# Two attention layers on one core: where the values of a step stand when an output product stands in it

## The chip, the cores and the metric

The kernel runs on one core of one Trainium2 chip. The metric is the device time of one execution in microseconds; of several runs the median is taken. A profile of one execution is at hand as well. In it PE is TensorE, PEld its weight loads, DVE is VectorE, ACT is ScalarE, POOL is GpSimd and SP is SyncE.

## The reference

Two attention layers run over two inputs of 2048 positions and 576 channels. Each has 32 heads of 18 channels. Their outputs stand side by side.

```python
def _A_ref(x, wqkv, wo):                 # local, dilated: 8 keys, 2 apart, back from the query
    ...
    logits = jnp.einsum("bhsd,bhswd->bhsw", q, kg) * scale
    attn = _softmax(jnp.where(mask[None, None, :, :], logits, -1e9), axis=-1)
    o = jnp.einsum("bhsw,bhswd->bhsd", attn, vg)
    return o.transpose(0, 2, 1, 3).reshape(B, S, D) @ wo

def _B_ref(x, wqkv, wo):                 # full attention
    ...
    p = _softmax(jnp.einsum("bhqd,bhkd->bhqk", q, k) * scale, axis=-1)
    o = jnp.einsum("bhqk,bhkd->bhqd", p, v)
    return o.transpose(0, 2, 1, 3).reshape(B, S, D) @ wo

return jnp.concatenate([a, b], axis=-1)
```

All tensors are float32.

## The kernel before

The work has three stages. First come the projections of both layers (to about 420 us). Then comes a long row of equal steps for the full attention of layer B, with layer A's local attention worked in beside it. The last part is an end with the last output products. The change touches the row of steps.

**A step.** There are 512 steps: 8 groups of 4 heads, in each 4 blocks of 512 queries, in each 16 tiles of 128 keys (`kt`). The order of instructions on each engine is the order in which the Python code issues them; a manual schedule is set, so nothing is moved afterwards. In a step TensorE does:

- four **scores** (`score`, matmul on L269): 128 keys by 512 queries, one for each head, of float32r. Heads 0 and 2 use the upper 64 rows of the array, heads 1 and 3 the lower 64, so that one of each kind run side by side. The order is `for h in (0, 2, 1, 3)`. ScalarE makes exponentials of each (`e`, L276).
- **maxima** for later blocks (`block`, matmul `take` on L158): scores of queries by keys, of which VectorE takes the maximum (`reduce`, L166, result `mx`). A step holds two whole ones (`maximum(1)` behind the first score, `maximum(0)` behind the last) and one in two halves of 256 columns that share one bank (`parts_of_maximum`). So three banks are reduced in each step. On VectorE the reduce of `maximum(1)` stands first, that of the two halves second, that of `maximum(0)` third.
- four **values** (`weigh`, L739): the exponentials of the step before, times the values `v`, summed into one bank `po` over 16 steps. Each is 19 columns wide, and the four stand in four column groups of the array. Each shows as two matmul records, so a step has eight.

**Banks.** `po` keeps one of eight PSUM banks. The other seven are handed out by `bank(kind)` in rings: the ring "scores" has banks 0 to 3, the ring "else" has banks 4 to 6. Each call gives the next bank of its ring; the matmul that writes it first waits until the bank's last reader is done.

**Output products.** When a part of a layer's attention is done, it is multiplied with `wo` (`beside`, matmul on L1058): two sums of 288 columns, `one` on the upper 64 rows and `two` on the lower, 13 or 14 matmuls each for layer A (27 in all), which run side by side. `one` takes a bank of the ring "scores", `two` one of "else". Two more maxima are put between its matmuls. `sums_of_a` does it for layer A (32 times), `sum_of` for layer B. A product that is due waits in the list `inside`, and the next step takes it in: before, just ahead of the step's last score (`h == 3`). In such a step the bank of `maximum(1)` is asked for first of all (`ps = bank() if inside and whole else None`), ahead of the bank of the two halves. Afterwards ScalarE copies one sum to `y` (L973) and VectorE adds the other (L974; issued from the list `behind_scores`).

**Values and exponentials.** At the end of each step the step before is weighed (`weigh(ready.pop(0))`), so two steps' exponentials are alive at once: eight tiles of 2 KB a partition, six in the pool `e_room` and two in `work`. Near the end, when there are no maxima left (`paired`), the values of two steps stand together.

**GpSimd's transfers.** 36 transfers are issued by GpSimd (L140, L141) in the projections; their descriptors lie in a scratch room of 16 KB a partition.

Of the kernel before, what the change touches and what calls it, by code (L numbers as in the profile page):

```python
# [7 lines left out]
F32 = mybir.dt.float32  # L8
F32R = mybir.dt.float32r
BF16 = mybir.dt.bfloat16  # L10
AF = mybir.ActivationFunctionType
# [22 lines left out]
ALL = NG * STEPS  # L34
# [25 lines left out]
def two_attentions(ctx: ExitStack, tc, xa, wa, woa, xb, wb, wob, out):  # L60
# [5 lines left out]
    nc = tc.nc  # L66
# [13 lines left out]
    def bank(kind=None):  # L80
        r = rings[kind or ring]
        r.append(r.pop(0))
        return p_bank.tile([128, 512], F32, name=f"bank{r[-1]}")
# [22 lines left out]
    step = 0  # L106
# [8 lines left out]
    def due():  # L115
        for f in agenda.pop(step, []):
            f()
# [89 lines left out]
    def settle():  # L207
        while owing:
            owing.popleft()()
# [7 lines left out]
    def next_piece(r):  # L217
        n, i = divmod(given[r], PIECES)
        given[r] += 1
        if n not in blocks:  # L220
            blocks[n] = block(*divmod(n, NB))
        return blocks[n], (r, i // 2 // NB, i // 2 % NB, i % 2)

    def maximum(r, ps=None):

        ps = ps or bank()
        (take, reduce), piece = next_piece(r)
        take(ps, *piece)
        return lambda: reduce(ps, *piece)
# [9 lines left out]
    def parts_of_maximum():  # L239

        if not begun:
            both = [next_piece(r) for r in range(2)]
            assert both[0][1][1:] == both[1][1][1:]
            begun.extend((both, part) for part in range(2))
        both, part = begun.popleft()
        ps = bank()
        one = both[1][0][0](ps, *both[1][1], part)

        between = nc.scalar.nop()
        sync(between, one)  # L250

        def other():
            (take, reduce), piece = both[0]
            sync(take(ps, *piece, part), between)
            reduce(ps, *piece, part)

        return other

    e_room = None
    counted = [-1]  # L260

    def score(g, b, kt, h, kind="scores", between=None):

        assert (g, b) in placed
        qs, ks = sets[g % 3]
        p, r = divmod(h, 2)
        ps = bank(kind)
        at = slice(64 * r, 64 * r + 56)
        nc.tensor.matmul(ps, ks[at, p, 128 * kt : 128 * kt + 128], qs[at, b, p], start=True, stop=True)  # L269
        if between:  # L270
            between()

        counted[0] += 1
        early = counted[0] % 8 < 6
        e = (e_room if early else work).tile([128, 512], F32, name="e", bufs=6 if early else 2)
        nc.scalar.activation(e, ps, AF.Exp, scale=SCALE)  # L276
        return e

# [26 lines left out]
    def halves(r, odd, w, x, wcols, xcols, weights_move=False):  # L305

        at = slice(64 * r, 64 * r + 64)
        both = [p for c in range(4) for p in pairs(c, w, x, wcols, xcols)] + pairs(4, w, x, wcols, xcols)[: 1 + (r == odd)]
        return [(b[at], a[at]) if weights_move else (a[at], b[at]) for a, b in both]
# [68 lines left out]
    with (tc.tile_pool(name="x", bufs=1, side="right") as xp,  # L378
# [4 lines left out]
        early = ExitStack()  # L383
# [98 lines left out]
        if True:  # L482
# [34 lines left out]
            for c in range(5):  # L517
                one, other = (load, nc.scalar.dma_start) if c % 2 == 0 else (nc.scalar.dma_start, load)
# [79 lines left out]
            for t in range(NT):  # L598
                ps = bank()
# [94 lines left out]
            for t in order[:4]:  # L694
                ps = bank()
# [34 lines left out]
        step = 0  # L730
# [3 lines left out]
    work = ctx.enter_context(tc.tile_pool(name="work", bufs=1, reuse_waits="tile"))  # L734
    ring = "else"
    def weigh(*steps):
        for g, b, kt, es in steps:
            for i in range(4):
                nc.tensor.matmul(po[32 * i : 32 * i + 19], vs[g][:, kt, 19 * i : 19 * i + 19], es[i],  # L739
                                 start=kt == 0, stop=kt == NT - 1)  # L740
        if kt == NT - 1:
            finish(g, b)
# [116 lines left out]
    def local(j):  # L859
# [102 lines left out]
        def finished(h, n):  # L962
            inside.append(lambda: sums_of_a(h, n))

        def sums_of_a(h, n):
            his, los = zip(*wo["a"])
            w = his[:4], los[:4], his[4], los[4]
            cols = slice(288 * h, 288 * h + 288)
            if h == 0:
                st["y"] = ys["a", j, n] = work.tile([128, D], F32, name="y", bufs=4)  # L970
            one, two = beside("scores", *(halves(r, 0, w, st["x", n], cols, slice(0, 128), True) for r in range(2)))
            y = st["y"][:, cols]
            nc.scalar.activation(y, two, AF.Copy)  # L973
            behind_scores.append(lambda: nc.vector.tensor_add(y, one, y))  # L974


        soon = 0 if j else 3
# [60 lines left out]
    behind_scores = []  # L1038

    inside = []  # L1040
# [3 lines left out]
    def beside(kind, *both):  # L1044

        sums_ = [bank(k)[:, :288] for k in (kind, None)]
        turns = [[(sums_[r], *ab, i == 0, i == len(t) - 1) for i, ab in enumerate(t)] for r, t in enumerate(both)]
        pair = kind and sum(given) + 2 <= NG * NB * PIECES * 2
        if pair:

            for r in range(2):
                turns[r].insert(6 + 4 * r, None)
        for i in range(max(map(len, turns))):
            for r in range(2):
                if i < len(turns[r]):
                    if turns[r][i]:
                        ps, a, b, start, stop = turns[r][i]
                        nc.tensor.matmul(ps, a, b, start=start, stop=stop)  # L1058
                    else:
                        maximum(r)()  # L1060
        if pair:

            rings["else"].append(rings["else"].pop(0))
        return sums_

    def sum_of(y, t, h, chunks, kind=None):

        pos, cols = slice(128 * t, 128 * t + 128), slice(288 * h, 288 * h + 288)
        both = []
        for r in range(2):  # L1070
            both.append([])
            for c, (hi, lo) in enumerate(chunks):
                at = slice(64 * r, min(64 * r + 64, hi.shape[0]))
                whi, wlo = wo["b"][c]
                both[r] += [(a[at, pos], w[at, cols]) for a, w in ((hi, whi), (hi, wlo), (lo, whi))]
        one, two = beside(kind, *both)
        if kind:
            nc.vector.tensor_copy(y, one)
        else:
            nc.scalar.activation(y, one, AF.Copy)  # L1080
        nc.vector.tensor_add(y, two, y)

    def first(t, b, h):
        sums[t, b, h] = bank()[:, :288]
# [40 lines left out]
    def partial(t, h):  # L1125

        b = NB - 1
        if h == 0:
            name = ("aq", "ao", "aohi")[t]
            ys["part", t] = work.tile([128, DH, SUB], F32, name=name, bufs=1)  # L1130
        y = ap(ys["part", t], (1, DH * SUB))[:, 288 * h : 288 * h + 288]
        waiting.append(lambda: sum_of(y, t, h, olds[b]))
        sums[t, b, h] = (y,)
# [22 lines left out]
    ready = [(0, 0, 0, es)]  # L1156
    early = sum(given)
# [4 lines left out]
    paired = False  # L1162
    due()
    step += 1
    while step < ALL:
        n, kt = divmod(step, NT)
        g, b = divmod(n, NB)
        es = [None] * 4

        whole = total - sum(given) > 1  # L1170
        parts = (bool(begun) or total - sum(given) > 3) and step not in copied

        ps = bank() if inside and whole else None


        ahead = kt == 0 and (n < 6 or n >= 24)
        part = [parts_of_maximum()] if parts and not ahead else []
        for h in (0, 2, 1, 3):

            if inside and h == 3:  # L1180
                inside.pop(0)()
            es[h] = score(g, b, kt, h, between=(lambda: part.append(parts_of_maximum())) if parts and ahead and h == 0 else None)
            if h == 0 and whole:
                maximum(1, ps)()
            if h == 1 and parts:
                part[0]()
            if h == 3 and whole:
                maximum(0)()
        if sum(given) == total and not begun:
            settle()  # L1190
        for fs in (behind_scores, outside):
            while fs:
                fs.pop(0)()

        paired = paired or kt % 2 == 0 and sum(given) == total and not begun
        for _ in range(1 if paired and step < ALL - 2 else len(waiting)):
            if waiting:
                waiting.pop(0)()
        if ready and (kt % 2 == 0 or not paired):
            weigh(ready.pop(0))  # L1200
        ready.append((g, b, kt, es))
        if paired and kt % 2:
            weigh(*ready)
            ready.clear()
        due()

        if len(waiting) > (0 if not paired else 2 if kt % 2 else len(waiting)):
            waiting.pop(0)()
        step += 1
# [24 lines left out]
```

## Time and profile before

| what | value |
|---|---|
| time, median of 3 runs | 1603.24 us (1603.08 to 1604.28) |
| span of the profiled execution | 1603.8 us; the page gives no other time for this execution |
| mean granted clock of TensorE | 0.998 |
| PE busy | 1590.0 us (99%) |
| DVE busy | 1383.7 us (86%) |
| ACT busy | 1217.7 us (76%) |
| POOL busy | 960.1 us (60%) |

The shares are means over stages. In the projections ACT is busy for 15 to 43 us of each 80 us; in the row of steps PE has 79 to 80 us of each 80, ACT 75 to 79 and DVE 74 to 76. In a row of the timeline the first number is the start in microseconds from the span's start, the second the duration; rows of equal instructions that follow each other are merged, and `x` counts them. In brackets stands the idle time of the engine ahead of the row, and what ended it.

### The profile page before, as it was taken

What the parts mean: (1) busy time and instruction counts of PE and PEld (TensorE: products, weight loads), DVE (VectorE), ACT (ScalarE), POOL (GpSimd) and SP (SyncE); (2) the same over time, 40 slices, a digit from 0 to 9 for tenths busy, and PEclk for the clock granted to TensorE, in tenths of its full rate; (3) what the DMA queues carried; (4) which work ended last, traced back from release to release, by engine and by line L of the source; (5) the groups of instructions that cost most, each with busy time, mean ns of one, the idle gap of its engine ahead of it and who ended that gap; (6) DMA issues with size and microseconds to landing.
All of it is one profiled execution on the core that took longest, in us unless ns stands there. A gap on an engine that the chain in (4) does not pass through costs nothing.

```text
span 1603.8 us, 35232 instructions
## 1 busy us (share of the span) xinstructions
PE 1590.0 (99%) x13388; PEld 950.3 (59%) x13388; DVE 1383.7 (86%) x2347; ACT 1217.7 (76%) x2438; POOL 960.1 (60%) x792
## 2 busy tenths in 40 slices
PE   9999999999999999999999999999999999999998
PEld 7999888999543444444444444444444444445676
DVE  5299899999999999999999999999999999999512
ACT  6423441221699999999999999999999999898655
POOL 2405742201166995896797897797797797772100
PEclk9999999999999999999999999999999999999999
DMA  8937954522312362254326325422632231144111
GB/s 247 235 125 199 258 173 124 162 92 80 74 37 67 72 143 72 59 133 99 73 76 143 74 78 131 105 78 61 135 100 65 65 96 32 50 163 157 62 39 60
DMA packets 186058, 172.11 MB, mean 107 GB/s; under 512 B 119152, under 2 KB 132976, under 8 KB 184160
## 3 DMA queue, kind: packets, MB, share of 16 engines
q1 hardware_dynamic: 181024, 158.31, 36.1%
q0 software_dynamic: 4032, 10.63, 3.1%
q8 instruction: 105, 1.72, 0.5%
q10 hardware_dynamic: 832, 0.92, 0.2%
q14 instruction: 65, 0.53, 0.1%
HBM read 96.94 MB, written 71.90 MB: 105 GB/s over the span
## 4 chain that ended last, share of the span: by engine, by line
PE 91%; DVE 4%; DMA 2%; ACT 2%; issue 0%; POOL 0%; SPq 0%; POOLq 0%; DVEq 0%; ACTq 0%
PE po L739 29%; PE bank L269 18%; PE bank L158 17%; PE bank L361 15%; PE bank L1058 8%; PE bank L298 5%; DVE mx L166 3%; ACT e L276 1%; DMA dqk<-olo 1%; DMA dqk<-ohi 1%; DMA den<-o 0%; POOL xlo L409 0%; PE bank L513 0%; DVE as L900 0%; ACT lg L909 0%
## 5 line engine op out<-in xcount | busy, mean ns | idle before, releaser
L166 DVE TENSOR_REDUCE mx<-bank 128x2 f32<-128x512 f32 x2048 | 1288.3, 684 | 110.5 <-PE bank L158 82.6
L276 ACT ACTIVATE e<-bank 128x512 f32<-128x512 f32 x2048 | 1049.9, 608 | 46.6 <-PE bank L269 43.3
L158 PE MATMUL bank<-ks,qs 54*128 54x256 f32 (+1 forms) x2530 | 787.7, 378 | 4.2 <-DVE mx L166 2.5
L158 PEld LDWEIGHTS bank<-ks,qs 54*128 54x128 f32 x2530 | 408.8, 184 | 445.7 <-DVE mx L166 397.0
L269 PE MATMUL bank<-qs,ks 56*128 56x512 f32 x2048 | 568.9, 426 | 0.0
L739 PE MATMUL po<-e,v 128*19 128x512 f32 x4096 | 537.7, 599 | 0.0
L269 PEld LDWEIGHTS bank<-qs,ks 56*128 56x128 f32 x2048 | 299.7, 184 | 29.3 <-ACT e L276 25.2
L882 POOL TENSOR_TENSOR pr<-aq,akv 128x1024 f32<-128x1024 f32 x72 | 158.3, 2200 | 15.8 <-DMA akv<-da 13.0
L925 POOL TENSOR_TENSOR pr<-lg,akv 128x1024 f32<-128x1024 f32 x72 | 158.3, 2199 | 0.6
L886 POOL TENSOR_TENSOR pr<-pr 128x1024 f32<-128x1024 f32 x64 | 152.6, 2384 | 5.0
L739 PEld LDWEIGHTS po<-e,v 128*19 128x19 f32 x4096 | 70.5, 97 | 129.1 <-issue 123.6
L689 ACT ACTIVATE ohi<-bank 128x512 f32<-128x512 f32 (+1 forms) x56 | 30.4, 595 | 150.8 <-issue 104.2
L361 PE MATMUL bank<-xhi,ahi 64*128 64x512 f32 (+1 forms) x448 | 114.3, 387 | 0.0
L361 PE MATMUL bank<-xhi,alo 64*128 64x512 f32 (+1 forms) x448 | 109.6, 387 | 0.0
L361 PE MATMUL bank<-xlo,ahi 64*128 64x512 f32 (+1 forms) x448 | 105.8, 388 | 0.1
L926 POOL TENSOR_TENSOR pr<-pr 128x512 f32<-128x512 f32 x72 | 92.4, 1284 | 5.6
L409 POOL TENSOR_TENSOR alo<-raw,ahi 128x512 fp32r<-128x512 f32 (+1 forms) x14 | 17.6, 1255 | 121.4 <-ACT ahi L408 113.2
L501 POOL TENSOR_TENSOR olo<-olo,ohi 128x512 fp32r<-128x512 f32 x36 | 46.2, 1294 | 70.9 <-ACT ohi L500 62.8
L101 POOL CAST mh<-mt 128x32 fp32r<-128x32 f32 x32 | 6.7, 210 | 101.5 <-DVE mt L183 96.3
L361 PEld LDWEIGHTS bank<-xhi,ahi 64*128 64x128 f32 (+1 forms) x448 | 64.1, 182 | 4.4
L499 ACT ACTIVATE olo<-bank 128x512 f32<-128x512 f32 x36 | 21.2, 589 | 56.4 <-PE bank L361 31.4
L361 PEld LDWEIGHTS bank<-xhi,alo 64*128 64x128 f32 (+1 forms) x448 | 60.2, 182 | 4.4
(203 smaller groups left out, 1846.2 us busy)
## 6 DMA issues: line engine op xcount, KB each, us to landing
do<-n SPq DMA_DIRECT2D x28, 512.0 KB
da<-ohi SPq DMA_DIRECT2D x52, 256.0 KB
akv<-da SPq DMA_DIRECT2D x64, 175.5 KB
out<-y SPq DMA_DIRECT2D x32, 288.0 KB
qs<-dqk SPq DMA_DIRECT2D x30, 288.0 KB
ks<-dqk SPq DMA_DIRECT2D x30, 288.0 KB
at<-dao SPq DMA_DIRECT2D x60, 128.0 KB
rec<-drec SPq DMA_DIRECT2D x29, 256.0 KB
```

Of the source, the lines that this page charges most:

```text
L158: return nc.tensor.matmul(ps if part is None else ps[:, 256 * r : 256 * r + 256], qs[at, b, p, 128 * t : 128 * t + 128], ks[at, p, 512 * k ...
L166: nc.vector.tensor_reduce(at, ps.rearrange("q (s n) -> q s n", s=2), axis=AX.X, op=ALU.max)
L269: nc.tensor.matmul(ps, ks[at, p, 128 * kt : 128 * kt + 128], qs[at, b, p], start=True, stop=True)
L276: nc.scalar.activation(e, ps, AF.Exp, scale=SCALE)
L298: nc.tensor.matmul(ps, a, b, start=c == i == 0, stop=c == 4 and i == 1)
L361: nc.tensor.matmul(ps, a, b, start=start, stop=stop)
L739: nc.tensor.matmul(po[32 * i : 32 * i + 19], vs[g][:, kt, 19 * i : 19 * i + 19], es[i], start=kt == 0, stop=kt == NT - 1)
L882: nc.gpsimd.tensor_mul(pr, ap(st["q"][:, 2 * c], (SUB, 2), (0, W), (1, SUB)), window(st["k"], c))
L886: nc.gpsimd.tensor_add(st["pr"], st["pr"], pr)
L925: nc.gpsimd.tensor_mul(at, ap(st["lg"], (0, 2), (SUB, W), (1, SUB)), window(st["v"], c))
L926: nc.gpsimd.tensor_add(at[:, :, :4], at[:, :, :4], at[:, :, 4:])
L1058: nc.tensor.matmul(ps, a, b, start=start, stop=stop)
```

## The change

- An output product that is due stands behind the step's four scores and its maxima, no longer ahead of the last score, and the bank of `maximum(1)` is no longer asked for ahead.
- Where a step has taken in an output product, `kt` is over 0, one step waits to be weighed, and the end is not near, the step weighs nothing (`later_values`); the next step then weighs both.
- So up to three steps' exponentials are alive: twelve tiles, six in each pool. The room for them comes from the descriptors' scratch room, which is halved.
- ScalarE copies `one` and VectorE adds `two`; before, it was the other way round in `sums_of_a`, and VectorE did both in some of `sum_of`'s.

```diff
-        early = counted[0] % 8 < 6
-        e = (e_room if early else work).tile([128, 512], F32, name="e", bufs=6 if early else 2)
+        early = counted[0] % 12 < 6
+        e = (e_room if early else work).tile([128, 512], F32, name="e", bufs=6)
...
-            nc.scalar.activation(y, two, AF.Copy)
-            behind_scores.append(lambda: nc.vector.tensor_add(y, one, y))
+            nc.scalar.activation(y, one, AF.Copy)
+            behind_scores.append(lambda: nc.vector.tensor_add(y, two, y))
...
         one, two = beside(kind, *both)
+        nc.scalar.activation(y, one, AF.Copy)
         if kind:
-            nc.vector.tensor_copy(y, one)
+            behind_scores.append(lambda: nc.vector.tensor_add(y, two, y))
         else:
-            nc.scalar.activation(y, one, AF.Copy)
-        nc.vector.tensor_add(y, two, y)
+            nc.vector.tensor_add(y, two, y)
...
-        ps = bank() if inside and whole else None
...
         for h in (0, 2, 1, 3):
-            if inside and h == 3:
-                inside.pop(0)()
             es[h] = score(g, b, kt, h, between=(lambda: part.append(parts_of_maximum())) if parts and ahead and h == 0 else None)
             if h == 0 and whole:
-                maximum(1, ps)()
+                maximum(1)()
             if h == 1 and parts:
                 part[0]()
             if h == 3 and whole:
                 maximum(0)()
+        later_values = False
+        if inside:
+            inside.pop(0)()
+            later_values = len(ready) == 1 and kt > 0 and step < ALL - 4 and not paired
...
-        if ready and (kt % 2 == 0 or not paired):
-            weigh(ready.pop(0))
+        if ready and (kt % 2 == 0 or not paired) and not later_values:
+            weigh(*ready)
+            ready.clear()
         ready.append((g, b, kt, es))
...
-    nc = bacc.Bacc("TRN2", target_bir_lowering=False, num_devices=1)
+    nc = bacc.Bacc("TRN2", target_bir_lowering=False, num_devices=1, dynamic_dma_scratch_size=8192)
```

In the built program's order of instructions 34 places have sixteen value matmuls (eight in the code) in one go that had twice eight before; 35 output products have their place moved. SP's and POOL's orders of instructions stay as they are.

## The prediction

> **What bounds the kernel now.** I read the page's busy times and its chain first.
>
> ```profile
> PE 1590.0 (99%) x13388; PEld 950.3 (59%) x13388; DVE 1383.7 (86%) x2347; ACT 1217.7 (76%) x2438; POOL 960.1 (60%) x792
> ...
> PE 91%; DVE 4%; DMA 2%; ACT 2%; issue 0%; POOL 0%; SPq 0%; POOLq 0%; DVEq 0%; ACTq 0%
> ...
> L166 DVE TENSOR_REDUCE mx<-bank 128x2 f32<-128x512 f32 x2048 | 1288.3, 684 | 110.5 <-PE bank L158 82.6
> L276 ACT ACTIVATE e<-bank 128x512 f32<-128x512 f32 x2048 | 1049.9, 608 | 46.6 <-PE bank L269 43.3
> L158 PE MATMUL bank<-ks,qs 54*128 54x256 f32 (+1 forms) x2530 | 787.7, 378 | 4.2 <-DVE mx L166 2.5
> L158 PEld LDWEIGHTS bank<-ks,qs 54*128 54x128 f32 x2530 | 408.8, 184 | 445.7 <-DVE mx L166 397.0
> ```
>
> TensorE is busy throughout and holds 91% of the chain. The 397.0 us "<-DVE" of L158 are idle time of the weight loader, which has nothing to load during the values; its matmuls sat idle for 4.2 us in all, 2.5 behind VectorE. ScalarE and VectorE wait for TensorE, not the other way. But busy shares don't tell by how much; the timeline of single steps does. Here is a plain step, to the start of the next:
>
> ```profile
> 609.25 0.39 PE L158 MATMUL bank<-ks,qs 54*128 54x256 f32 x1
> ...
> 609.48 0.40 PE L158 MATMUL bank<-ks,qs 54*128 54x512 f32 x1
> ...
> 609.95 0.44 PE L269 MATMUL bank<-qs,ks 56*128 56x512 f32 x1
> 609.97 0.42 PE L158 MATMUL bank<-ks,qs 54*128 54x512 f32 x1
> 610.31 1.05 PE L739 MATMUL po<-e,v 128*19 128x512 f32 x8
> 611.30 0.38 PE L158 MATMUL bank<-ks,qs 54*128 54x256 f32 x1
> ```
>
> It takes 2.05 us: 1.06 for scores and maxima, 0.99 for values, no gap. Now a step with an output product, from its first matmul (603.07) to the next step's (607.23):
>
> ```profile
> 603.07 0.38 PE L158 MATMUL bank<-ks,qs 54*128 54x256 f32 x1
> ...
> 603.77 0.53 PE L1058 MATMUL bank<-wohi,at 64*128 64x288 f32 x4
> ...
> 604.64 0.40 PE L158 MATMUL bank<-ks,qs 54*128 54x512 f32 x1
> ...
> 605.20 0.39 PE L158 MATMUL bank<-ks,qs 54*128 54x512 f32 x1
> ...
> 605.82 0.40 PE L269 MATMUL bank<-qs,ks 56*128 56x512 f32 x1
> ...
> 605.93 0.39 PE L158 MATMUL bank<-ks,qs 54*128 54x512 f32 x1
> ...
> 606.03 0.41 ACT L973 ACTIVATE y<-bank 128x288 f32<-128x288 f32 x1 [0.84 <-PE bank L1058]
> ...
> 606.25 1.05 PE L739 MATMUL po<-e,v 128*19 128x512 f32 x8
> ...
> 606.96 0.45 DVE L974 TENSOR_TENSOR y<-bank,y 128x288 f32<-128x288 f32 x1
> ...
> 607.23 0.38 PE L158 MATMUL bank<-ks,qs 54*128 54x256 f32 x1
> ...
> 609.25 0.39 PE L158 MATMUL bank<-ks,qs 54*128 54x256 f32 x1
> ```
>
> The product takes 2.05 us (603.77 to 605.82) and TensorE doesn't wait. With the plain step behind it that is 6.18 us (603.07 to 609.25). This pair is what the change rearranges, in 34 places.
>
> **Standing two steps' values together: a gain.** The profiled execution has such rows already, near the end:
>
> ```profile
> 1514.89 1.91 PE L739 MATMUL po<-e,v 128*19 128x512 f32 x16
> 1516.73 0.40 PE L1058 MATMUL bank<-qs,pr 64*128 64x288 f32 x2
> ```
>
> Sixteen records hold TensorE for 1.84 us, twice eight for 2 x 0.98 = 1.96 (606.25 to 607.23). Leaving the values once less saves 0.12. Entering them takes 0.32 to 0.34 from the last maximum's start (605.93 to 606.25, 609.97 to 610.31) where a 512-column pair otherwise follows after 0.23 (609.25 to 609.48): 0.10 more. The new order without any wait would then be 0.94 (scores and maxima, 0.71 + 0.23), 2.05 (product), 1.06 (next step's) and 1.84: 5.89 us for the pair, 0.29 less than 6.18. The 0.07 above 0.12 + 0.10 is the product's odd matmul, which no longer keeps one half of the array idle ahead of a switch; I keep it.
>
> **Moving the product behind the maxima: a wait.** This is where I choose. The product's second sum asks for the next bank of the ring of three. Before, the bank of the first maximum was fetched early, so the ring gave the product the bank of the previous step's last maximum, long reduced. Now the step takes its three banks in the plain order (two halves, first maximum, last maximum), and the product's is the fourth: the bank of the two halves of this very step. VectorE reduces that one second. The built order of instructions shows it at every product (the first one: the halves in bank 6, the maxima in 4 and 5, the product's second sum in 6, with a wait for VectorE). When that bank is free, the product step of before tells:
>
> ```profile
> 603.72 0.69 DVE L166 TENSOR_REDUCE mx<-bank 128x2 f32<-128x512 f32 x1
> ...
> 604.33 0.68 DVE L166 TENSOR_REDUCE mx<-bank 128x2 f32<-128x512 f32 x1
> ...
> 603.61 0.60 ACT L276 ACTIVATE e<-bank 128x512 f32<-128x512 f32 x1
> ...
> 1482.52 1.28 DVE L166 TENSOR_REDUCE mx<-bank 128x2 f32<-128x512 f32 x2
> ...
> 1483.26 0.38 PE L158 MATMUL bank<-ks,qs 54*128 54x256 f32 x1 [0.38 <-DVE mx L166]
> ```
>
> Counted from 603.07, the second reduce ends at 1.94. TensorE goes on 0.06 after the reduce that it waits for (the first of the two from 1482.52 ends at 1483.20, the matmul starts at 1483.26), so the lower half of the product starts at 2.00, where TensorE is ready at 0.94. The upper half's bank, of the ring of scores, comes free with the first exponential at 603.61 + 0.60, that is 1.14, plus 0.06: its first matmul slips in ahead, the rest is queued behind the waiting one. Everything on TensorE is: the two maxima in the product, the next step. The product ends at 2.00 + 2.05 - 0.10 (the matmul that slipped in) = 3.95 in place of 2.99: **0.96 us lost**. Nothing covers it: TensorE has no slack, and VectorE can't be quicker, since both its reduces of that step run back to back.
>
> **What is late next.** The product's second maximum starts 1.42 after the product (603.77 to 605.20 above), so at 3.42, and ends at 3.81; its reduce starts about 0.04 later, ends at 4.53, and its bank goes to the next step's first maximum at 4.59, which wants it at 3.95 + 0.23 = 4.18: **0.41 lost**. That step's last maximum stands 0.49 behind (609.48 to 609.97), at 5.08. It now takes the bank of the product's second sum, which VectorE frees with the addition to `y`, and that follows ScalarE's copy: the product's last matmul ends near 4.2, copy 0.41 to 4.65, addition 0.45 to 5.11, free at 5.17: **0.09 lost**. Values start 0.34 later and end at 5.17 + 0.34 + 1.84 = 7.35. Against 6.18 a pair costs 1.17 more: -0.29 + 0.96 + 0.41 + 0.09.
>
> **Edits at no cost.** Twelve tiles for eight: exponentials wait for TensorE's scores (43.3 of 46.6 us, above), so a tile more gains nothing; it covers the third step's exponentials, which would otherwise stand behind 1.84 us of values. The swap of engines at `y` keeps copy and addition, and moves the release of banks, counted above. The sixteen records in one go let VectorE run dry: three banks hold 3 x 0.61 = 1.8 us of reduces (603.72 to 604.33 is 0.61). It finds all banks empty afterwards, and TensorE is not behind; I price it at nothing, with up to 0.3 a pair at the upper end (about half a reduce). The smaller descriptor room touches 36 transfers of the projections:
>
> ```profile
> POOL ks L140 <- DMA qs<-dqk: 5.4, 3, 3.1
> ...
> POOL vs L586 <- DMA dv<-vs: 13.1, 1, 13.1
> ```
>
> GpSimd waited 5.4 us for landings there and sat idle for 13.1 right afterwards, so a second such wait would be covered; nothing, and up to 5 us if it isn't.
>
> **The sum.** 34 x 1.17 = 39.8, and one of the places holds two products, whose second wait adds 0.96: +40.7 us. On the profiled span of 1603.8 that is 1644.5; the median of the runs lies 0.6 lower at 1603.24, so 1644. The lower end takes the first wait alone: 34 x (0.96 - 0.29) = 23, 1626. The upper end adds 0.3 a pair: 40.7 + 10 = 51, and rounded up for the transfers, 1656.
>
> **Rivals.** *Only the gain*: 34 x 0.29 = 9.9 us less, 1593. It needs the product to find its bank free, and decides once the added wait stays under 0.29 a pair. For it: TensorE alone bounds, and its switches are real. Against it: two reduces take 1.3 us whatever TensorE does, and the halves' last 256 columns come late in the step. I give it 0.08. *Gain and waits cancel*, within 0.2% of before (about what a measurement of this kernel can tell from no change): waits of 0.2 to 0.4 a pair, for which no row speaks: 0.02.
>
> *The clock falls.* New idle time on TensorE can cost more than itself:
>
> ```profile
> 177.90:180.10 2.20, 0.00 (x0) 0.00 (x0) 0.45 (x1) 0.61 (x2) 0.47 (x1) 1.00 1.02 338
> ...
> 181.35:184.77 3.42, 3.42 (x18) 2.97 (x17) 2.29 (x4) 2.44 (x4) 3.34 (x5) 0.50 0.66 192
> ...
> 502.18 0.38 PE L158 MATMUL bank<-ks,qs 54*128 54x256 f32 x1 [0.70 <-DVE mx L166]
> ...
> 480.00:560.00 80.00, 79.00 (x612) 32.25 (x610) 75.11 (x130) 78.74 (x156) 65.95 (x62) 1.00 0.29 69
> ```
>
> Here 2.2 us without a matmul were followed by 3.42 us at a granted clock of 0.50; 0.70 us idle were not (1.00 over its stretch). My first wait, 1.06 with a matmul in it, lies between, nearer to the 0.70. If each pair lost half of 3.42 us, that is 34 x 1.7 = 58 more, 1702; at every second pair 1673. I give it 0.07. The Trainium skill ("TensorE: Matmul & The Clock Gate", Part 1) has it that the gate looks at free-running windows of about 3.4 us and halves the clock after an idle one. By that rule no wait of this change is long enough, and the sum stays; the trace agrees on 3.42 us of half clock, but shows that 2.2 us idle are enough.
>
> That the change doesn't do what it says is excluded by the built order.
>
> **How the numbers follow.** The forecast with its bounds, 1626 to 1656, holds 0.83; the gain 0.08, the draw 0.02, the clock 0.07. Slower is forecast and clock together, 0.90. The range leaves out 0.17.
>
> **What would show it.** Right: idle time of about 1 us ahead of the L1058 matmuls in 35 places, put down to DVE mx; some 0.4 us ahead of L158 in the step behind; rows of sixteen L739 that hold TensorE for 1.84. Wrong: product steps without a gap, or a granted clock under 1.00 behind them; gaps in the steps that have no product.

## The result, and the profile after

The changed kernel takes 1649.39 us (median of 4 runs, 1648.28 to 1650.3), the kernel before beside it 1603.53 us. The ratio is 1.0286, with a 95% interval of 1.0271 to 1.03: 45.9 us slower. Forecast were 1644 us, range 1626 to 1656.

The profiled execution has a span of 1648.5 us, 44.7 more than before, at a granted clock of 0.999. The page's busy line, its chain, and two groups of instructions of the changed kernel:

```profile
PE 1614.5 (98%) x13388; PEld 959.0 (58%) x13388; DVE 1381.6 (84%) x2344; ACT 1218.1 (74%) x2441; POOL 959.7 (58%) x792
...
PE 83%; DVE 8%; ACT 3%; POOL 2%; DMA 2%; issue 1%; SPq 1%; POOLq 0%; DVEq 0%
...
L158 PE MATMUL bank<-ks,qs 54*128 54x256 f32 (+1 forms) x2530 | 791.2, 379 | 7.4 <-DVE mx L166 3.0
...
L1058 PE MATMUL bank<-wohi,at 64*128 64x288 f32 x480 | 70.3, 310 | 14.8 <-ACT e L276 9.8 <-DVE mx L166 3.1 <-DMA qs<-dqk 0.4
```

VectorE and ScalarE have taken a part of the chain (DVE 4% to 8%, ACT 2% to 3%), and the products now wait. But the idle time shows less than half of it. Of the 44.7 us only 20.2 are idle time of TensorE (1648.5 - 1614.5 against 1603.8 - 1590.0); the other 24.5 are booked as busy. TensorE counts as busy while one half of the array has a matmul, even if the other half's next matmul, and with it everything behind, waits.

The timeline of TensorE over the first pair, from 602.07, shows where the time is (VectorE's and ScalarE's rows after it):

```profile
602.07 0.38 PE L158 MATMUL bank<-ks,qs 54*128 54x256 f32 x1
...
602.78 0.38 PE L158 MATMUL bank<-ks,qs 54*128 54x512 f32 x1
603.30 0.37 PE L1058 MATMUL bank<-wohi,at 64*128 64x288 f32 x1
604.07 0.52 PE L1058 MATMUL bank<-wohi,at 64*128 64x288 f32 x3 [0.40 <-DMA akv<-da]
...
605.49 0.39 PE L158 MATMUL bank<-ks,qs 54*128 54x512 f32 x1
...
606.12 0.34 PE L158 MATMUL bank<-ks,qs 54*128 54x256 f32 x1
606.20 0.39 PE L269 MATMUL bank<-qs,ks 56*128 56x512 f32 x1
606.68 0.50 PE L158 MATMUL bank<-ks,qs 54*128 54x512 f32 x1
...
607.35 0.50 PE L158 MATMUL bank<-ks,qs 54*128 54x512 f32 x1
607.78 1.91 PE L739 MATMUL po<-e,v 128*19 128x512 f32 x16
609.62 0.38 PE L158 MATMUL bank<-ks,qs 54*128 54x256 f32 x1
```

```profile
602.73 0.69 DVE L166 TENSOR_REDUCE mx<-bank 128x2 f32<-128x512 f32 x1
...
603.33 0.68 DVE L166 TENSOR_REDUCE mx<-bank 128x2 f32<-128x512 f32 x1
...
605.94 0.68 DVE L166 TENSOR_REDUCE mx<-bank 128x2 f32<-128x512 f32 x1
...
606.40 0.41 ACT L973 ACTIVATE y<-bank 128x288 f32<-128x288 f32 x1 [1.72 <-PE bank L1058]
...
606.84 0.46 DVE L974 TENSOR_TENSOR y<-bank,y 128x288 f32<-128x288 f32 x1 [0.22 <-ACT y L973]
```

The second reduce ends at 604.01; the product goes on at 604.07, 2.00 after the step's start, where without a wait it could have gone on at 0.94. One matmul of the upper half slipped in at 603.30, so of these 1.06 us only 0.14 ahead of it and 0.40 behind it are idle. The row names a DMA as releaser, which does not fit: in other products the same gap is put down to VectorE's reduce, and the runs below that move this reduce, or the bank that it frees, move the product. In 19 of the 32 products of layer A the upper half's matmul slips in only at 1.57 or later, behind a later first exponential, and runs until about the end of the reduce. There the idle time is put down to ScalarE, and the wait for the reduce hardly shows: 9.8 of the 14.8 us ahead of L1058 stand under ScalarE, 3.1 under VectorE.

The reduce of the product's second maximum ends at 606.62, the next step's first maximum starts at 606.68. The addition to `y` ends at 607.30, the last maximum starts at 607.35. The pair ends 7.55 after its start.

Worked out from the starts in the trace, 32 pairs with a product of layer A have a median of 7.52 us, where before a product step (4.13) and the step behind it (2.02) took 6.15: 1.37 more each. Over the 32 pairs that adds up to 43.9 us (240.9 against 196.9). Behind the last of them, where layer B's products stand, 3.0 us are lost as well; ahead of the first and between them 2.2 are gained. Together these are the 44.7.

### The profile page after: what moved, and what is told of

It is laid out like the page before. It is cut to its first block, busy times and chain, and to the rows that moved or that the text cites. A ratio compares the mean times of both kernels' runs of the same rounds, so it can differ in the third digit from the quotient of the medians.

```text
span 1648.5 us, 35198 instructions
## 1 busy us (share of the span) xinstructions
PE 1614.5 (98%) x13388; PEld 959.0 (58%) x13388; DVE 1381.6 (84%) x2344; ACT 1218.1 (74%) x2441; POOL 959.7 (58%) x792
## 4 chain that ended last, share of the span: by engine, by line
PE 83%; DVE 8%; ACT 3%; POOL 2%; DMA 2%; issue 1%; SPq 1%; POOLq 0%; DVEq 0%
PE po L739 27%; PE bank L158 16%; PE bank L269 15%; PE bank L361 15%; DVE mx L166 7%; PE bank L1058 6%; PE bank L298 5%; ACT e L276 2%; POOL pr L925 1%; POOL xlo L409 1%; DMA qs<-dqk 1%; DMA dqk<-olo 1%; ACT o L749 0%; POOL pr L926 0%; SPq L506 0%
## 5 line engine op out<-in xcount | busy, mean ns | idle before, releaser
L739 PE MATMUL po<-e,v 128*19 128x512 f32 x4096 | 531.0, 598 | 0.0
L739 PEld LDWEIGHTS po<-e,v 128*19 128x19 f32 x4096 | 74.0, 97 | 141.2 <-issue 136.1
L1058 PE MATMUL bank<-wohi,at 64*128 64x288 f32 x480 | 70.3, 310 | 14.8 <-ACT e L276 9.8
L1058 PEld LDWEIGHTS bank<-wohi,at 64*128 64x128 f32 x480 | 52.0, 185 | 30.3 <-ACT e L276 19.6
```

## The experiments

Two theories stand against each other. Mine says that the new place of the product costs, through banks: TensorE waits for the reduce of a bank, and behind the product for the way out of the product's own banks (copy and addition). The rival says that the pairing itself costs, sixteen value matmuls in one go. All times are medians beside the kernel before on the same chip (1603.9 to 1604.2 us).

**The product moved, the values not.** The changed kernel with

```diff
-            later_values = len(ready) == 1 and kt > 0 and step < ALL - 4 and not paired
+            later_values = False
```

> The changed kernel, but every step weighs as before: only the product's place and its banks move. Bank theory: each of 35 products waits for the reduce of the halves of its own step, as in the changed kernel (starts 2.00 us after the step, not 0.94), and the values behind it hide the later waits: about +1.0 us each, 35 us in all, near 1638 us. Rival, the values: if sixteen value matmuls in one go (VectorE running dry) are what costs, the time is back near 1604.

Measured: 1639.23 us, 1.0225 (1.0209 to 1.024). So 35 of the 46 us come with the place alone. The first product step starts here:

```profile
600.59 0.38 PE L158 MATMUL bank<-ks,qs 54*128 54x256 f32 x1
...
601.83 0.37 PE L1058 MATMUL bank<-wohi,at 64*128 64x288 f32 x1
602.59 0.52 PE L1058 MATMUL bank<-wohi,at 64*128 64x288 f32 x3 [0.39 <-DMA akv<-da]
...
604.80 1.05 PE L739 MATMUL po<-e,v 128*19 128x512 f32 x8
```

In 32 product steps the product goes on at 2.00 and the step takes 5.17 us (4.13 before): 1.04 each. The step behind takes 2.01, as before: with the values between, the later waits are covered.

**The values paired, the product in its old place.** The kernel before with twelve tiles, 8 KB and

```diff
+        later_values = False
...
             if inside and h == 3:
                 inside.pop(0)()
+                later_values = len(ready) == 1 and kt > 0 and step < ALL - 4 and not paired
...
-        if ready and (kt % 2 == 0 or not paired):
-            weigh(ready.pop(0))
+        if ready and (kt % 2 == 0 or not paired) and not later_values:
+            weigh(*ready)
+            ready.clear()
```

> The kernel before with the values of two steps together behind each product, twelve tiles and 8 KB, but the product in its old place, ahead of the last score, with its old banks. Bank theory: no wait at the product; the values no longer give VectorE time between the product's maxima and the next step's, so the next step's first halves wait 0.27 us for the second maximum's reduce and its third score about 0.7 us for the addition to y, less 0.29 for the switch saved: +0.6 a pair, near 1625 us. Rival, only the gain: 34 x 0.29 less, near 1594. Rival, the values cost by themselves: near 1649.

Measured: 1625.64 us, 1.014 (1.0125 to 1.0155). Pairing loses without the move, too. The chain of it, in TensorE's timeline and in its waits:

```profile
601.02 0.38 PE L158 MATMUL bank<-ks,qs 54*128 54x256 f32 x1
...
603.79 0.39 PE L269 MATMUL bank<-qs,ks 56*128 56x512 f32 x1
603.87 0.87 PE L158 MATMUL bank<-ks,qs 54*128 54x512 f32 x2
604.36 0.49 PE L269 MATMUL bank<-qs,ks 56*128 56x512 f32 x1
...
605.41 0.49 PE L269 MATMUL bank<-qs,ks 56*128 56x512 f32 x1 [0.33 <-DVE y L974]
...
606.05 1.91 PE L739 MATMUL po<-e,v 128*19 128x512 f32 x16
607.90 0.38 PE L158 MATMUL bank<-ks,qs 54*128 54x256 f32 x1
```

```profile
PE bank L269 <- DVE y L974: 10.5, 32, 0.4
```

The third score of the step behind the product starts 4.39 after the pair's start, behind the addition to `y`; such a wait stands in 32 places. Sixteen value matmuls hold TensorE for 1.85 us (606.05 to 607.90): the switch is saved, and less than the wait. The losses of these two runs, 35 and 22 us, don't add up to 46. In this one the bank that the addition frees is wanted by the next step's third score; in the changed kernel, with other banks, only by its last maximum.

**That wait taken away.** The kernel above with VectorE's addition left out for layer A, so half of each of its products is missing from the output:

```diff
             nc.scalar.activation(y, two, AF.Copy)
-            behind_scores.append(lambda: nc.vector.tensor_add(y, one, y))
```

> The kernel with pairs and the product in its old place (e2), with VectorE's addition of the second sum left out for layer A: half of each of its products is missing from the output. The bank of that sum is then free as soon as the product ends. Theory: in e2 it is the way out of the product's banks (copy, then addition) that the next step waits for, since no values stand behind the product any more; without it the third score doesn't wait, 0.65 less a pair, near 1605 us. Rival, the extra values or the reduces: it stays near 1625.

Measured: 1607.61 us, 1.0024 (1.0014 to 1.0034): 18 of the 22 us are gone. The scores no longer wait:

```profile
L269 PE MATMUL bank<-qs,ks 56*128 56x512 f32 x2048 | 567.9, 425 | 0.0
```

So it is the way out of the product's bank that values behind a product cover. But even without it the pair doesn't win: 6.26 us in the median, 6.15 before. By the trace of the first pair, the next step begins 0.48 behind the step's last maximum (603.56 to 604.04) in place of 0.23, as it waits for the reduce of the product's second maximum, and the values enter 0.42 behind the last maximum (604.75 to 605.17) in place of 0.34. These 0.33 are more than the 0.22 (0.12 and 0.10) that were forecast for the switch.

**The way out made shorter.** The kernel with pairs and the product in its old place, with

```diff
-            nc.scalar.activation(y, two, AF.Copy)
-            behind_scores.append(lambda: nc.vector.tensor_add(y, one, y))
+            nc.scalar.activation(y, one, AF.Copy)
+            nc.vector.tensor_add(y, two, y)
```

> The kernel with pairs and the product in its old place (e2), with the way out of the product's banks made shorter: ScalarE copies the first sum, and VectorE's addition is issued straight behind the product, ahead of the reduce of the step's last maximum. If the way out is what the pair waits for, its second bank comes free at 3.9 us after the step in place of 4.4, the last maximum's reduce is 0.5 later in turn: W starts near 4.86 in place of 5.00, about 0.15 less a pair than e2, near 1621 us. If it were the values, 1625 as e2. By neither is it under the kernel before.

Measured: 1626.12 us, 1.0138 (1.0124 to 1.0152): nothing gained against 1625.64, where I expected 5 us. The row for it, in place of the 10.5 us above:

```profile
PE bank L158 <- DVE y L974: 5.4, 30, 0.3
```

The wait has changed its matmul. The next step's first maximum now waits for the addition. The addition also stands ahead of the last maximum's reduce and holds that one back, whose bank the next step's last maximum needs. The values start at 4.99 (5.01 without this edit; medians of 32 pairs) where 4.86 was expected.

**Another bank for the product.** The changed kernel with the first maximum's bank asked for ahead again, so that the product's second sum gets the bank that is reduced first:

```diff
+        ps = bank() if inside and whole else None
...
-                maximum(1)()
+                maximum(1, ps)()
```

> The changed kernel with the bank of the first maximum asked for ahead again in a product's step; nothing else. The product's second sum then takes the bank that VectorE reduces first. Bank theory: it starts 1.41 us after the step in place of 2.00, the waits behind it stay: 0.59 less a pair, near 1630 us. Rival, the place or the values as such: no change against 1649.

Measured: 1634.39 us, 1.0192 (1.0175 to 1.0209): 15 us of the loss go with one line that moves no work. That is 4 us less than expected, and the trace says why. In 11 of the 32 places the product goes on at 1.40, as worked out. In the other 21 it goes on at about 1.60: there the first exponential comes at about 0.90 in place of 0.54, since ScalarE copies `po` just ahead, and the upper half's bank is late. The copies are this row of the instruction groups of the kernel before, which the single place that I had looked at doesn't show:

```profile
L749 ACT ACTIVATE o<-po 128x512 f32<-128x512 f32 x23 | 14.6, 635 | 1.6 <-PE po L739 1.6
```

**Both sums in the ring of scores.** The changed kernel with

```diff
-        sums_ = [bank(k)[:, :288] for k in (kind, None)]
+        sums_ = [bank(k)[:, :288] for k in (kind, kind)]
...
-            rings["else"].append(rings["else"].pop(0))
+            pass
```

> The changed kernel with both sums of a product in banks of the ring of scores. Bank theory: the product waits for the step's second exponential in place of the second reduce (1.68 us after the step, about 2.04 where ScalarE has copied po just before), the next step's first maximum no longer waits, but its last score waits about 0.5 for the addition to y: 0.3 to 0.5 less a pair, 1632 to 1639 us, and the idle time ahead of L1058 is put down to ACT e alone. Rival, the place or the values as such: no change against 1649.

Measured: 1644.85 us, 1.0257 (1.0242 to 1.0273): a gain of 4.5, under what I expected, and only 1.5 of it lies in the 32 pairs (239.3 us against 240.9). The places differ as above. In the 11 with an early exponential the product goes on at 1.67 (1.68 was worked out) and a pair takes 7.24. In the 21 others it goes on at about 2.08, later than in the changed kernel, and a pair takes 7.60. The row of L1058 no longer names the reduce, which had 3.1 us in the changed kernel; the exponentials' share, 9.9, is as it was there:

```profile
L1058 PE MATMUL bank<-wohi,at 64*128 64x288 f32 x480 | 70.6, 310 | 13.4 <-ACT e L276 9.9
```

**VectorE's order changed, TensorE's not.** The changed kernel; in a step with a product the halves are reduced first:

```diff
             if h == 0 and whole:
-                maximum(1)()
+                reduce_first = maximum(1)
+                if not (inside and parts and not ahead and whole):
+                    reduce_first()
             if h == 1 and parts:
                 part[0]()
+                if inside and not ahead and whole:
+                    reduce_first()
```

> The changed kernel; in a product's step VectorE reduces the halves ahead of the first maximum, and nothing else is moved. Bank theory: the halves are through on TensorE at 0.87, their reduce ends at 1.60 in place of 1.94, the product starts at 1.66 us after the step in place of 2.00, the waits behind it stay: 0.35 a pair less, near 1637 us. Rival, TensorE's own order costs (place, balance of the two halves of the array): 1649, as TensorE's instructions are the same.

Measured: 1639.03 us, 1.0219 (1.0204 to 1.0235): 10.4 less than the change, with TensorE's instructions as they were.

```profile
601.08 0.38 PE L158 MATMUL bank<-ks,qs 54*128 54x256 f32 x1
...
605.36 0.50 PE L158 MATMUL bank<-ks,qs 54*128 54x512 f32 x1
...
606.46 1.91 PE L739 MATMUL po<-e,v 128*19 128x512 f32 x16
608.30 0.38 PE L158 MATMUL bank<-ks,qs 54*128 54x256 f32 x1
```

The product goes on at 1.67 in both kinds of place (1.66 was worked out), the next step's first maximum at 4.28 (601.08 to 605.36) in place of 4.61, and a pair takes 7.22. So these 10.4 us are not TensorE's own order, but what it waits for.

**A quicker reduce.** Both kernels with VectorE reading half of each bank:

```diff
-            nc.vector.tensor_reduce(at, ps.rearrange("q (s n) -> q s n", s=2), axis=AX.X, op=ALU.max)
+            nc.vector.tensor_reduce(at, ps.rearrange("q (s n) -> q s n", s=2)[:, :, :128], axis=AX.X, op=ALU.max)
```

> The kernel before, VectorE reducing 256 of each bank's 512 columns (the maxima are of half the keys): the reference for the next one. TensorE bounds, so 1600 to 1605 us by every theory.

> The changed kernel with the same halved reduces. If the reduces were the whole of the loss, the gain would show: 34 x 0.29 under the one before, near 1593 us. My theory: the product waits until 1.46 to 1.60 in place of 2.00 (the halves' reduce, or the first exponential), the maxima's wait goes, but the way out of the product's bank (copy and addition, 0.95 us behind the product) then stops the next step's last maximum for about 0.5: 0.8 a pair above before, near 1632 us.

Measured: 1595.51 and 1628.08 us, 0.9949 (0.9934 to 0.9964) and 1.0154 (1.0139 to 1.0169) of the kernel before. A reduce takes 421 ns in place of 684, and the change still costs 32.6 us, 0.96 a pair: a quicker VectorE takes away some 13 of 46 us. What is left is the first exponential (the product goes on at 1.46 or 1.59) and the way out of the banks: in the first pair the addition ends at 601.19, and the next step's last maximum starts at 601.24. The kernel before with halved reduces is the quickest of all, and 4.5 us quicker than the least that I expected. It starts the row of steps at 417.3 us, not 422.9; about 1.7 of these 5.6 us (an estimate, half of 3.42) are not VectorE's, as the profile before has 3.42 us at half the clock in its projections (from 181.35) and this one has none. So VectorE limits in the projections as well. It takes its maxima over half of the keys, though, so it isn't the same guard against large exponents, and has nothing to do with this change.

```profile
L166 DVE TENSOR_REDUCE mx<-bank 128x2 f32<-128x256 f32 x2048 | 781.3, 421 | 591.0 <-PE bank L158 561.6 <-PE bank L361 10.8 <-PE bank L269 0.8
```

**The edits priced at nothing.** The kernel before with twelve tiles, 8 KB of descriptor room and the swap at `y` (in `sum_of` too, as in the changed kernel):

```diff
-        early = counted[0] % 8 < 6
-        e = (e_room if early else work).tile([128, 512], F32, name="e", bufs=6 if early else 2)
+        early = counted[0] % 12 < 6
+        e = (e_room if early else work).tile([128, 512], F32, name="e", bufs=6)
...
-            nc.scalar.activation(y, two, AF.Copy)
-            behind_scores.append(lambda: nc.vector.tensor_add(y, one, y))
+            nc.scalar.activation(y, one, AF.Copy)
+            behind_scores.append(lambda: nc.vector.tensor_add(y, two, y))
```

> The kernel before with the edits that I priced at nothing: twelve tiles of exponentials, 8 KB of descriptor room, ScalarE copying the first sum and VectorE adding the second. The product's place and the values stay. Mine: within 2 us of the kernel before, 1602 to 1606. Rival: one of them has a price (a transfer of GpSimd that waits for room, a bank that comes free later), 1608 or more.

Measured: 1607.25 us, 1.0022 (1.0012 to 1.0032): 3.3 us, small but clear of zero. It sits in the step behind each product:

```profile
604.76 0.38 PE L158 MATMUL bank<-ks,qs 54*128 54x256 f32 x1
...
604.99 0.49 PE L158 MATMUL bank<-ks,qs 54*128 54x512 f32 x1
...
606.87 0.38 PE L158 MATMUL bank<-ks,qs 54*128 54x256 f32 x1
```

That step takes 2.11 us here, 2.02 before (607.23 to 609.25), and 32 times 0.10 is the 3.3 us. The bank from the ring of maxima is now freed by VectorE's addition, later than by ScalarE's copy, and the next step's first maximum wants it. The trace fits this: the addition ends at 604.94, that maximum starts at 604.99 and takes 0.49 in place of 0.40. No run has the swap alone. Tiles and descriptor room show no price: the row of steps starts at 420.4 us, and before at 422.9, or about 421.2 without the 1.7 for half the clock.

None of these arrangements with pairs, or with the product behind the maxima, beats the kernel before.

## Why the prediction was right

The size was forecast at 1644, 5.4 us under what was measured, and the steps held in their order.

- **The bank of the halves.** Expected at 2.00 after the step, measured 2.00, in all 32 products of layer A. Handing out another bank (1634), or reducing that one earlier (1639), moves the time with it. Shown. The sign that was named for it came otherwise: not about 1 us of idle time put down to VectorE, but 14.8 us in all, most of it under ScalarE, since the upper half's matmul that slips in hides the rest.
- **The later waits.** The next step's first maximum was expected at 4.59 and came at 4.61 (602.07 to 606.68). The last one was expected at 5.17 and came at 5.28. The way out of the product's bank counts for more than I gave it where nothing stands ahead of it, as the two kernels with pairs and the product in its old place show (18 us).
- **The terms mis-sized.** The matmul that slips in ahead saved nothing: the product took 2.05 to 2.13 us from 604.07 to the next step's first matmuls at 606.12 and 606.20, not 1.95. That moves the copy and the addition by about 0.1, and the values start 0.43 behind the last maximum (607.35 to 607.78), not 0.34. Together that is 0.20 of the pair's 1.37 against my 1.17, and 34 x 0.20 = 6.8 us is the difference to 1644 and a little more.
- **The gain.** Sixteen value matmuls hold TensorE for 1.84 us (607.78 to 609.62), as expected. It never shows as a net gain, as every pair measured here has waits that are longer.
- **The swap at `y`** was priced only through the release of a bank, 0.09 a pair. In the kernel before, together with the tiles and the descriptor room, it costs 3.3 us, where values stand between and I expected no price. No run takes it out of the changed kernel, so what it adds there stays open.
- **The rivals.** Only the gain, and gain and waits that cancel: refuted by 45.9 us. The clock: 1.00 from 420 to 1520 us in the changed kernel, so 1.06 us of waiting with a matmul in it did not lower it here.
- **One place for all.** The waits were worked out at one place. For the changed kernel it did not matter, since the reduce comes last in both kinds of place; that was luck, and for two experiments it did matter.
- **What stays argued.** No run takes away all waits at once, and the split of the pair's 1.37 into its terms is read from the timeline.

## What to carry to other kernels

Where buffers are handed out in a ring, moving a piece of work past others changes which buffer it gets. Write down the ring's order around the moved piece and ask who reads its buffer last, before pricing the move; one early request for a bank was worth 15 us here. Work that looks like an overhead between two stages (values behind each product) can be the cover under which another engine empties buffers, and joining it elsewhere takes the cover away.

## What the runs showed of the hardware that was not expected

TensorE's idle time in the profile understates a wait where the two halves of the array run different matmuls: of 44.7 us lost, 24.5 are booked as busy.

The length of a gap alone does not tell whether the granted clock falls. In the kernel before, 2.2 us without a matmul were followed by 3.42 us at half the clock, and in the changed kernel 1.73 us (173.41 to 175.14) by 3.41 us of it, from 175.85. In the kernel with pairs and the product in its old place, 1.86 us without a matmul (from 173.80) were followed by none. The 32 waits of 1.06 us with one matmul in them left it at 1.00.
